# Moving the scalings of the Down weights inside a block, and re-ordering the first step with attention

## The chip, the cores and the metric

The kernel runs on one core of a Trainium2 chip. The core has five engines that follow their own queues of instructions: TensorE (PE in the profile; its weight loads are PEld), VectorE (DVE), ScalarE (ACT), GpSimd (POOL) and SyncE (SP), which here issues the transfers. The metric is the device time of one execution in microseconds, as the median of several runs.

## The reference

A layer mixes two branches by a gate. Tokens: 2048, width 576, 32 heads of 18, four segments of 512 tokens, hidden width 4608:

```python
g = sigmoid((x * gate_w).sum(-1, keepdims=True))
a = A(x, wq, wk, wv, wo, beta)                # causal softmax attention inside each segment, mixed per
                                              # head with a read of a memory summed over earlier segments
b = (gelu(x @ w_gate) * (x @ w_up)) @ w_down  # GEGLU feed-forward
return g * a + (1 - g) * b
```

Attention in a segment is `softmax(q k^T * scale + mask) @ v`; the memory adds `phi(k)^T v` of each segment for the later ones.

## The kernel before, in words

**Words and scales.** All large products are made of float16 words: each float32 operand is scaled by a power of two and split into a high word and the low word that is left, and a product is three matmuls (high by high, high by low, low by high). The scale comes from the sum of squares of the operand.

**Blocks and steps.** After a first part (projections, memory), the main loop runs over 72 steps v (`step`, L1455). The 4608 hidden columns are 36 slices of 128; two slices make a block fb (18 blocks of four steps, i4 = 0 to 3), and a step takes one slice f = v // 2 and one half of the tokens (two chunks of 512). "Third step" below means i4 = 2, the first step of a block's second slice. Each step forms gate and up values for two chunks by a scheme with seven block products instead of eight; its operands are sums of weight blocks and sums of token blocks, and its results are built up in three banks called V, X (bank G) and Y (bank U). Y starts as a copy of X (L1504 in the first two steps of a block, L1507 in the others), X and Y are then continued with different products (`product`, L533; `rest` and `half_rest` for the last 64 columns of the width). VectorE reads Y twice on the way (L1558 or L1560 for the first chunk, L1598 for the second) and V once (L1606); a product that goes on in a bank waits until VectorE has read it. ScalarE makes the GELU (L1323), VectorE the gated value (`hidden`, L1305), ScalarE its high word (L1312), GpSimd its low word (L1320).

**The nested product.** In the fourth step of a block and the first of the next, one of the seven products is itself made by such a scheme, with 256 columns a matmul (`nest`, L1408, four parts n = 0 to 3 in one bank V of two halves). VectorE copies and adds between the parts: L1421 after part 0, L1424 and L1425 after part 1 (part 2 goes on in both halves that L1425 reads and writes), L1429 after part 2, L1432 after part 3. In the first block this happens with `at = (1, 1)` in step v = 4.

**Down products.** The hidden values of block fb - 1 are multiplied with its Down weights during block fb: 32 chains of six matmuls with 288 columns (`down`, L1272, by `chains` / `some`), eight in a step, five of them "early", three "late". Each chain ends in one of two dn banks and VectorE adds it to the result (L1290; L1288 in block 1).

**Attention.** From v = 4 on, step v carries one head of one half sequence, k = v - 4, for 64 steps (`on(k)`): the scores of two segments (`scores`, L1170, matmuls L1190, in banks dn, st and pv), VectorE's masked maxima (L1196, started by `put`), the exponentials and words on ScalarE and GpSimd (`powers`, L1203: L1210, L1214, L1215, L1216), transposes by SyncE (L1219), the products with v (`values`, L1221, bank pv) and `normalize` (L1236, last instruction L1250). The scores of step k need bank pv after `normalize` of k - 2 has read it.

**Preparation of weights.** While a block runs, the weights of the next are scaled on VectorE (`scale_g`, L314), summed on GpSimd (`sums_g`, L337 to L342; `nest_odd`, `nest_pairs`, `nest_sums`, L375 to L397) and split (`high_g`, L348 on ScalarE; `low_g`, L352 on GpSimd). The Down weights of the block itself (`raw_d`, two slices) come in during its first step, ScalarE sums their squares in its second (L89), `scale_d` (L399, instruction L401) scales them in place on VectorE, `high_d` (L403, instruction L405) makes the upper half on ScalarE, `low_d` (L407, instruction L409) the lower half on GpSimd in the fourth step. They are used from the next block on.

**Order.** The order of the instructions on TensorE, ScalarE, VectorE and GpSimd is the order in which the code emits them (a manual schedule); semaphores are set from the data that they share. SyncE's transfers go in order too. So a line's place in `step` is its place in its engine's queue: `weights_nest(fb, i4, 2)` is the end of a step, and `end_pair` (L1443) the start of the next.

Of the kernel before, what the change touches and what calls it, by code (L numbers as in the profile page):

```python
# [27 lines left out]
NB = NF // 2  # L28
# [15 lines left out]
def kernel(ctx: ExitStack, tc: tile.TileContext, xs, wqk, wv, wo, wgu, wd, beta, out):  # L44
# [234 lines left out]
    def scales_rest(fb):  # L279
        z, pb = scl_a[fb]  # L280
        dve.tensor_scalar(pb[:, 0, 0:2].bitcast(I32), z[:, 4:6].bitcast(I32), 1, EXP, OP.logical_shift_right, OP.bitwise_and)
        dve.tensor_scalar(pb[:, 0, 2:6].bitcast(I32), z[:, 0:4].bitcast(I32), EXP, None, OP.bitwise_and)
        dve.tensor_scalar(pb[:, 1].bitcast(I32), pb[:, 0].bitcast(I32), EXP, None, OP.bitwise_xor)
# [24 lines left out]
    A11, A12, U4, A22, G4, S1, UG, S2, S4 = 0, 2, 4, 5, 7, 8, 10, 11, 13  # L308
    KW = KT * P

    def scale_g(f, cols=slice(0, KT * P)):
        if f < NF:
            r = raw_g[f].rearrange("p (a b) -> p a b", a=2)[:, :, cols]
            dve.tensor_scalar(r, r, scl[f // 2][0][:, 0:1], None, OP.mult)  # L314
# [16 lines left out]
    def sums_g(f):  # L331
        if f >= NF:
            return
        r = raw_g[f]
        g0, g2, u0, u2 = (r[:, o : o + 2 * P] for o in (0, 2 * P, KW, KW + 2 * P))
        g4, u4 = r[:, 4 * P : KW], r[:, KW + 4 * P :]
        pool.tensor_tensor(g2, g0, g2, OP.add)  # L337
        if f < 2 or f % 2 == 0:
            pool.tensor_tensor(g0, u0, g0, OP.subtract)
        pool.tensor_tensor(u0, g2, u0, OP.subtract)  # L340
        pool.tensor_tensor(u2, u2, u0, OP.subtract)
        pool.tensor_tensor(g4, u4, g4, OP.subtract)  # L342
# [23 lines left out]
    def nest_part(b):  # L366

        w = nest_w[b][:, 10 * P :].bitcast(F32)
        return raw_g[2 * b][:, : 2 * P], w

    def nest_odd(b):
        if b < NB:
            nest_w[b] = nest_tile()
            r = raw_g[2 * b + 1]
            pool.tensor_tensor(nest_part(b)[1], r[:, KW : KW + 2 * P], r[:, : 2 * P], OP.subtract)  # L375

    def nest_pairs(b, i, what):
        if b >= NB:
            return
        a, r = nest_part(b)  # L380
        src, o = ((a, W00), (r[:, P:], W11), (r, WS3), (a, WS2))[i]
        n = src.shape[1]
        hi, lo = (nest_w[b][:, (o + 7 * j) * P : (o + 7 * j) * P + n] for j in range(2))
        if "h" in what:
            act.activation(hi, src, AF.Copy)
        if "l" in what:
            pool.tensor_tensor(lo, src, hi, OP.subtract)
# [11 lines left out]
    def scale_d(f):  # L399
        r = raw_d[f]  # L400
        dve.tensor_scalar(r, r, scl[f // 2 + 1][0][:, 1:2], None, OP.mult)  # L401

    def high_d(f):  # L403
        t = pair_d[f] = home["d"].tile([P, 2, D], F16, name="paird", tag="paird", bufs=4)
        act.activation(t[:, 0], raw_d[f], AF.Copy)  # L405
# [127 lines left out]
    def product(o, f, a, x, h, l, start=False, ks=(0, 1)):  # L533

        w = pair_g[f]
        for k in ks:
            for i, b in ((0, h), (0, l), (1, h)):
                pe.matmul(o, w[:, i, (a + k) * P : (a + k + 1) * P], x[:, b + k],  # L538
                          start=start and k == 0 and i == 0 and b == h, stop=k == 1 and i == 1,
                          skip_group_check=True)  # L540
# [20 lines left out]
    with tc.tile_pool(name="prj", bufs=2, side="right", reuse_waits="tile") as pp:  # L561
# [262 lines left out]
        with tc.manual_schedule(engines=ORDERED):  # L824
# [43 lines left out]
            x1 = [pp.tile([P, L], F32, name="phi", bufs=9) for _ in range(2)]  # L868
# [253 lines left out]
    with tc.tile_pool(name="keep", bufs=2, side="right", reuse_waits="tile") as kp, ExitStack() as tail:  # L1122
# [222 lines left out]
                scale_g(n0 + 2)  # L1345

        def weights_nest(fb, i4, at):
            if i4 == 1 and at == 2 and 0 < fb < NB - 1:
                for f in (2 * fb, 2 * fb + 1):
                    scale_d(f)  # L1350
            if i4 == 2 and at == 1:
                if fb:
                    scale_g(2 * fb + 3, FRONT)
                    sums_g(2 * fb + 2)
                nest_odd(fb + 1)
            if i4 == 2 and at == "late":
                for i in range(2):
                    nest_pairs(fb + 1, i, "hl")
                nest_sums(fb + 1)
            if i4 == 2 and at == 2:  # L1360
                for i in (2,) if fb else (2, 3):
                    nest_pairs(fb + 1, i, "hl")
            if i4 == 3 and at == 0 and fb:
                nest_pairs(fb + 1, 3, "hl")

        def weights_high(fb, i4):
            n0 = 2 * fb
            high_g(n0 + 1 + i4 // 2, i4 % 2)
            if i4 >= 2:
                high_d(n0 + i4 - 2)  # L1370

        def weights_low(fb, i4):
# [35 lines left out]
        def nest(at, n):  # L1408

            if at is None:  # L1410
                return
            b, p = at
            if n == 0:
                nested[at] = bank("V")
                holds[p] = kp.tile([P, L], F32, name=f"hold{p}", bufs=1)
            B, A = (nested[at][:, i * HX : (i + 1) * HX] for i in range(2))
            h0, h1 = (holds[p][:, i * HX : (i + 1) * HX] for i in range(2))
            if n == 0:
                nest_product(b, B, W00, X00, p, True)
                nest_product(b, A, WS3, XT3, p)  # L1420
                dve.tensor_copy(h1, A)  # L1421
            if n == 1:
                nest_product(b, A, W11, XT4, p)
                dve.tensor_copy(h0, A)  # L1424
                dve.tensor_copy(A, B)  # L1425
            if n == 2:
                nest_product(b, B, W01, X10, p)
                nest_product(b, A, WS2, XT2, p)
                dve.tensor_tensor(h0, A, h0, OP.add)  # L1429
            if n == 3:  # L1430
                nest_product(b, A, WS1, XT1, p)
                dve.tensor_tensor(h1, A, h1, OP.add)  # L1432
# [22 lines left out]
        def step(v):  # L1455

            f, p = divmod(v, 2)
            fb, i4 = divmod(v, 4)
            c, e = 2 * p, 2 * p + 1
            k = v - LAG  # L1460
            on = lambda i: 0 <= i < 2 * H
            early = range(8 * i4, 8 * i4 + 5)
            late = range(8 * i4 + 5, 8 * i4 + 8)
            some = lambda b, js: chains(b, js) if b >= 0 else None
# [4 lines left out]
            x1, x2_, t = x16[c], x16[e], xt[p]  # L1469
# [8 lines left out]
            at = (fb + 1, 0) if i4 == 3 and fb + 1 < NB else (fb, 1) if i4 == 0 and fb else None  # L1478
# [7 lines left out]
            X, Y = bank("G"), bank("U")  # L1486
# [88 lines left out]
                scales_out(fb + 1)  # L1575
            if both and i4 != 1:
                normalize(k - 2)
            product(X, f, A12, x1, 2, 6, ks=(0,) if on(k) else (0, 1))
            if v != 3 and not on(k):
                rest(X, f, U4, x1, (0,) if fb else (0, 1))  # L1580
            if fb > 1 and i4 == 1:
# [7 lines left out]
                rest(X, f, U4, x1)  # L1589
            if on(k):  # L1590
                scores(k, (f, V, G4, x1, 0), (f, X, U4, x1, 0), (f, Y, G4, x2_, 64))
                product(X, f, A12, x1, 2, 6, ks=(1,))
                rest(X, f, U4, x1, (0,))
            elif fb:
                low_rests(f, (V, G4, x1), (Y, G4, x2_))
# [16 lines left out]
            if on(k) and i4 == 1:  # L1612
                scales_sum(fb + 1, pool)
                scales_rest(fb + 1)
            rear = list(early[3 + (v == 4) :])
            if not on(k):
                some(fb - 1, rear)
# [18 lines left out]
            if on(k):  # L1636
                some(fb - 1, rear[:-1])
                nest(at, 0)
                some(fb - 1, rear[-1:])
                nest(at, 1)  # L1640
                put(2 * k + 1, 1)
                puts.pop(2 * k)
                weights_nest(fb, i4, "late")
                powers(2 * k)
                some(fb - 1, late[:1])
                ends.append((f, c, X, g0))
                end_first()
                some(fb - 1, late[1:2])
                nest(at, 2)
                some(fb - 1, late[2:])  # L1650
                if on(k - 1):
                    values(2 * k - 2)
                nest(at, 3)
            else:
                if v != 3:
                    nest(at, 0)
                some(fb - 1, late[:1])
                if v != 3:
                    nest(at, 1)
                weights_nest(fb, i4, "late")  # L1660
                some(fb - 1, late[1:])
                if v != 3:
                    nest(at, 2)
                if fb:
                    low_rests(f, (X, U4, x1), (Y, UG, x2_))
                    ends.append((f, c, X, g0))
                    if at or i4 == 1:
                        end_first()
                if on(k - 1):
                    values(2 * k - 2)  # L1670
                if v != 3:
                    nest(at, 3)
# [160 lines left out]
        with tc.manual_schedule(engines=ORDERED):  # L1833
# [17 lines left out]
            fb = NB - 1  # L1851
            for t in range(turned_n, 9):
                turned(t)
            for t in range(16):
                for n in range(2):
                    down(fb, t, n)
                if t in (1, 4):
                    f, c, o, g = ends.pop(0)
# [82 lines left out]
```

## Time and profile before

| | |
|---|---|
| Runs before | 1564.15, 1564.54, 1564.54 us (median 1564.54) |
| Profiled execution | 1564.22 us, span 1562.1 us |
| TensorE (PE) busy | 1550.3 us, 99% of the span |
| VectorE (DVE) busy | 1257.6 us, 81% |
| ScalarE (ACT) busy | 1210.0 us, 77% |
| GpSimd (POOL) busy | 1123.9 us, 72% |
| Granted TensorE clock | 1.000 |

Rows of a timeline read: start in us from the span's start, duration in us, engine, line of the kernel, operation, output tile <- input tiles, partitions x elements and type, and x with the number of instructions that the row merges. In square brackets stands the time that the engine was idle before the row and what ended it. Rows of the waits read: engine, tile and line that waited <- what it waited for: total us, times, longest us. The row of one line's instructions gives the shortest, median and longest duration in ns, then the first and the last start. Since matmuls are pipelined, the duration of a matmul row includes time in which the next one already runs; the distance between two starts is the pace.

### The profile page before, as it was taken

Reading aid. Unit: us, or ns where it says so; the run is one execution under the profiler, and the core shown is the slowest. Engines: PE = TensorE matmul, PEld = TensorE weight load, DVE = VectorE, ACT = ScalarE, POOL = GpSimd, SP = SyncE. Lnnn points to the kernel's source line nnn. Section 1 sums busy time; section 2 is a strip of 40 time slices with the busy share of each in tenths; the row PEclk is TensorE's granted clock in tenths of the full one; section 3 lists DMA queues with packets and bytes.
Section 4 is the critical chain, followed back from the end, with each engine's and each line's share of the span. In section 5 each row is a group of like instructions: output and inputs, shape, how many; then the busy total and the mean of one; then the engine's idle time right before and its main releaser. Section 6 shows DMA issues by size and latency. Waiting matters only on the chain. (4 is left out here: it accounts for less than half of the span.)

```text
span 1562.1 us, 33442 instructions
## 1 busy us (share of the span) xinstructions
PE 1550.3 (99%) x12196; PEld 967.7 (62%) x12196; DVE 1257.6 (81%) x3222; ACT 1210.0 (77%) x2059; POOL 1123.9 (72%) x1233
## 2 busy tenths in 40 slices
PE   9999999999999999999999999999999999999999
PEld 5765655565656666666666565666666666656577
DVE  7878986888888888888788888888888878887675
ACT  7567545898989888888889888989888888877421
POOL 4355566777777778686877777777878686777597
PEclk9999999999999999999999999999999999999999
DMA  7644441465747576656656584757576666655646
GB/s 246 235 153 146 155 133 41 106 133 102 146 109 149 112 154 119 138 127 124 135 117 136 107 154 106 149 111 165 113 146 123 123 139 126 129 104 102 122 91 168
DMA packets 483477, 206.69 MB, mean 132 GB/s; under 512 B 427248, under 2 KB 462320, under 8 KB 482800
## 3 DMA queue, kind: packets, MB, share of 16 engines
q1 hardware_dynamic: 483312, 204.56, 58.6%
q8 instruction: 95, 1.56, 0.4%
q14 instruction: 70, 0.57, 0.1%
HBM read 83.91 MB, written 31.98 MB: 74 GB/s over the span
## 5 line engine op out<-in xcount | busy, mean ns | idle before, releaser
L538 PEld LDWEIGHTS <-pairg 128*128 128x128 f16 x2592 | 242.5, 97 | 266.0 <-issue 23.8
L1280 PE MATMUL dn<-paird,hhr 128*128 128x288 f16 x2115 | 329.9, 286 | 0.2
L1290 DVE SCALAR_TENSOR_TENSOR acc<-dn,ev,acc 128x288 f32<-128x288 f32 x533 | 267.6, 513 | 76.8 <-PE dn L1280 74.4
L1214 ACT ACTIVATE pb<-pb,mb,esc 128x512 f32<-128x512 f32 (+3 forms) x512 | 304.9, 642 | 5.3
L1216 POOL TENSOR_TENSOR pb<-pb,ph 128x896 f16<-128x896 f32 (+1 forms) x128 | 187.7, 1467 | 118.6 <-ACT ph L1215 94.7
L1216 POOL TENSOR_TENSOR pl<-pb,ph 128x896 f16<-128x896 f32 (+1 forms) x128 | 180.6, 1431 | 120.4 <-ACT ph L1215 120.4
L1280 PEld LDWEIGHTS <-hhr 128*128 128x128 f16 x2160 | 210.2, 98 | 74.5 <-issue 1.3
L538 PE MATMUL G<-x,pairg 128*128 128x512 f16 x864 | 221.0, 380 | 0.0
L538 PE MATMUL U<-xt,pairg 128*128 128x512 f16 x864 | 209.9, 379 | 4.5 <-DVE U L1507 4.3
L1280 PE MATMUL dn<-paird,hhd 128*128 128x288 f16 x1275 | 208.7, 286 | 0.0
L1215 ACT ACTIVATE ph<-pb 128x896 f16<-128x896 f32 (+1 forms) x256 | 188.6, 737 | 9.6
L352 POOL TENSOR_TENSOR pairg<-raw,pairg 128x384 f16<-128x384 f32 (+2 forms) x144 | 157.6, 1115 | 17.2 <-ACT pairg L348 17.2
L1280 PEld LDWEIGHTS <-hhd 128*128 128x128 f16 x1296 | 125.6, 98 | 47.4 <-issue 0.5
L1405 PE MATMUL V<-xt,nest 128*128 128x256 f16 x714 | 105.5, 272 | 0.6 <-DVE hold L1429 0.4
L538 PE MATMUL U<-x,pairg 128*128 128x512 f16 x432 | 105.0, 379 | 0.0
L538 PE MATMUL V<-x,pairg 128*128 128x512 f16 x426 | 103.3, 378 | 0.1
L1196 DVE CUSTOM_DVE_ANT_0 pb<-st,mask 128x128 f32<-128x128 f32 (+2 forms) x192 | 96.5, 503 | 0.0
L1323 ACT ACTIVATE gl<-gl,sc 128x512 f32<-128x512 f32 x110 | 75.2, 712 | 26.0 <-DVE gl L1598 13.7
L1196 DVE CUSTOM_DVE_ANT_0 pb<-dn,mask 128x512 f32<-128x512 f32 (+2 forms) x192 | 92.1, 505 | 0.0
L1233 PEld LDWEIGHTS <-pt 128*128 128x128 f16 x2560 | 83.3, 96 | 6.5 <-issue 0.2
L419 PEld LDWEIGHTS <-wp 128*128 128x128 f16 x504 | 48.8, 98 | 59.0 <-DVE wp L115 1.0
L348 ACT ACTIVATE pairg<-raw 128x384 f16<-128x384 f32 (+2 forms) x144 | 77.8, 587 | 8.9 <-DVE raw L314 6.5
(367 smaller groups left out, 3213.7 us busy)
## 6 DMA issues: line engine op xcount, KB each, us to landing
raw<-in_wgu_dram SPq DMA_DIRECT2D x36, 640.0 KB
qkt<-qk SPq DMA_DIRECT2D x192, 108.0 KB
rawd<-in_wd_dram SPq DMA_DIRECT2D x36, 288.0 KB
qk<-stage SPq DMA_DIRECT2D x32, 256.0 KB
qk<-stage SPq DMA_DIRECT2D x40, 128.0 KB
vp<-vstage SPq DMA_DIRECT2D x16, 296.0 KB
vt<-vp SPq DMA_DIRECT2D x16, 296.0 KB
orow<-oa SPq DMA_DIRECT2D x16, 288.0 KB
```

The costliest lines, as they stand in the source:

```text
L348: act.activation(spot(f, *p, 0), raw_g[f][:, p[0] : p[1]], AF.Copy)
L352: pool.tensor_tensor(spot(f, *p, 1), raw_g[f][:, p[0] : p[1]], spot(f, *p, 0), OP.subtract)
L538: pe.matmul(o, w[:, i, (a + k) * P : (a + k + 1) * P], x[:, b + k], start=start and k == 0 and i == 0 and b == h, stop=k == 1 and i == 1, ...
L1196: dve.tensor_tensor_reduce(scored(u, qi), out[u, qi], mask[:, L - (qi + 1) * P :], 1.0, -3e38, OP.add, OP.max, mx[u][:, qi : qi + 1])
L1214: act.activation(r, r, AF.Exp, bias=b[:, qi : qi + 1], scale=esc[:, 0, c : c + 1])
L1215: act.activation(h[:, cols], p, AF.Copy)
L1216: pool.tensor_tensor(low[:, cols], p, h[:, cols], OP.subtract)
L1233: pe.matmul(ov, pr[:, 10 * i + COL[qi] // P + kb], v[:, 4 * e + kb, c0 : c0 + VC], start=kb == 0 and i == 0, stop=kb == qi and i == 1)
L1280: pe.matmul(o[:, :NH], hh[:, a, q * P : (q + 1) * P], w[:, b, n * NH : (n + 1) * NH], start=i == 0, stop=i == 5)
L1290: dve.scalar_tensor_tensor(av, o[:, :NH], ev, av, OP.mult, OP.add)
L1323: act.activation(t, o, AF.Gelu_apprx_tanh, scale=scl[f // 2][0][:, 2 + c : 3 + c])
L1405: pe.matmul(o, w[:, (7 * c + i) * P : (7 * c + i + 1) * P], x[d], start=start and n == 0, stop=n == 2, skip_group_check=True)
```

## The change

Three things are moved; no computation is added or taken away.

- In blocks 1 to 16, the two scalings of the block's Down weights (`scale_d`) leave the end of the second step. The first of them stands in the third step behind the maxima of the scores, the second at the third step's end.
- In the same blocks, the upper half of the first Down slice (`high_d(2 * fb)`) moves from the middle of the third step to its end. The second slice's stays in the fourth step, as do both lower halves. The last block keeps its order.
- In the first step with attention (v = 4, k = 0), X's second group of three matmuls stands right behind the first, ahead of the scores, and the first "late" Down chain stands ahead of part 1 of the nested product instead of behind it.

```diff
         def weights_nest(fb, i4, at):
-            if i4 == 1 and at == 2 and 0 < fb < NB - 1:
-                for f in (2 * fb, 2 * fb + 1):
-                    scale_d(f)
             if i4 == 2 and at == 1:
...
             if i4 == 2 and at == 2:
                 for i in (2,) if fb else (2, 3):
                     nest_pairs(fb + 1, i, "hl")
+                if 0 < fb < NB - 1:
+                    high_d(2 * fb)
+                    scale_d(2 * fb + 1)
             if i4 == 3 and at == 0 and fb:
                 nest_pairs(fb + 1, 3, "hl")
 
         def weights_high(fb, i4):
             n0 = 2 * fb
             high_g(n0 + 1 + i4 // 2, i4 % 2)
-            if i4 >= 2:
+            if i4 == 3 or (i4 == 2 and fb == NB - 1):
                 high_d(n0 + i4 - 2)
...
-            product(X, f, A12, x1, 2, 6, ks=(0,) if on(k) else (0, 1))
+            product(X, f, A12, x1, 2, 6, ks=(0,) if k > 0 and on(k) else (0, 1))
...
             if on(k):
                 scores(k, (f, V, G4, x1, 0), (f, X, U4, x1, 0), (f, Y, G4, x2_, 64))
-                product(X, f, A12, x1, 2, 6, ks=(1,))
+                if k:
+                    product(X, f, A12, x1, 2, 6, ks=(1,))
                 rest(X, f, U4, x1, (0,))
...
             if on(k) and i4 == 1:
                 scales_sum(fb + 1, pool)
                 scales_rest(fb + 1)
+            if on(k) and i4 == 2:
+                scale_d(2 * fb)
...
                 some(fb - 1, rear[:-1])
                 nest(at, 0)
                 some(fb - 1, rear[-1:])
+                if k == 0:
+                    some(fb - 1, late[:1])
                 nest(at, 1)
                 put(2 * k + 1, 1)
                 puts.pop(2 * k)
                 weights_nest(fb, i4, "late")
                 powers(2 * k)
-                some(fb - 1, late[:1])
+                if k:
+                    some(fb - 1, late[:1])
```

## The prediction

> **What bounds the kernel now.** I read the page's head first, then the waits of TensorE, then the timeline of one block of the steady part (block 12, whose third step begins near 1092 us) engine by engine.
>
> ```profile
> span 1562.1 us, 33442 instructions
> ```
>
> The profiled execution took 1564.22 us, so 2.1 us lie around the span; the three runs have 1564.15, 1564.54 and 1564.54, so my sum, made against 1564.22, may read 0.3 us low against the median. TensorE is busy 99% of the span. What a re-ordering can win is therefore only what TensorE still waits for.
>
> ```profile
> PE U L538 <- DVE U L1507: 4.3, 16, 0.8
> ...
> PE V L1405 <- DVE hold L1429: 0.4, 1, 0.4
> ```
>
> One wait comes back 16 times, once in each block from 1 to 16: product Y of the third step waits for the copy of X into Y's bank. Idle time understates it, because a matmul's modelled end overlaps the next start. I therefore measure from start to start:
>
> ```profile
> 1093.75 1.46 PE L538 MATMUL G<-x,pairg 128*128 128x512 f16 x6
> ...
> 1096.28 0.38 PE L1328 MATMUL V<-x,pairg 128*128 128x512 f16 x1
> 1096.89 1.46 PE L538 MATMUL U<-xt,pairg 128*128 128x512 f16 x6 [0.23 <-DVE U L1507]
> ...
> 1101.91 0.39 PE L1332 MATMUL V<-x,pairg 64*128 64x512 f16 x1
> 1102.33 0.27 PE L1190 MATMUL pv<-qkt 54*128 54x256 f16 x1
> ...
> 1105.69 3.91 PE L1280 MATMUL dn<-paird,hhd 128*128 128x288 f16 x30
> ...
> 1113.77 0.38 PE L1328 MATMUL V<-x,pairg 128*128 128x512 f16 x1
> 1113.98 1.46 PE L538 MATMUL U<-xt,pairg 128*128 128x512 f16 x6
> ...
> 1119.01 0.39 PE L1332 MATMUL V<-x,pairg 64*128 64x512 f16 x1
> 1119.23 0.27 PE L1190 MATMUL pv<-qkt 54*128 54x256 f16 x1
> ```
>
> The fourth step (last four rows) shows the undisturbed pace: 0.21 us from V's rest to Y, 0.22 us from the half rest to the first score. The third step needs 0.61 and 0.42 us. So two stalls stand in each third step: 0.40 us at the copy, and 0.20 us at the scores, which no wait of the table names. VectorE is behind both:
>
> ```profile
> 1092.59 0.51 DVE L401 TENSOR_SCALAR rawd<-rawd,sc 128x576 f32<-128x576 f32 x1
> 1093.02 2.15 DVE L401 TENSOR_SCALAR rawd<-rawd,sc 128x576 f32<-128x576 f32 x1
> ...
> 1096.14 0.70 DVE L1507 COPY U<-G 128x512 f32<-128x512 f32 x1
> ...
> 1098.25 0.88 DVE L314 TENSOR_SCALAR raw<-raw,sc 128x1280 f32<-128x1280 f32 x1
> 1099.05 0.68 DVE L1558 TENSOR_TENSOR gl<-U,hold 128x512 f32<-128x512 f32 x1
> ...
> 1101.88 0.30 DVE L1250 TENSOR_TENSOR ob<-ob,pv 128x144 f32<-128x144 f32 x1
> ...
> 1105.01 0.42 DVE L1196 CUSTOM_DVE_ANT_0 pb<-pv,mask 128x256 f32<-128x256 f32 x1
> ...
> 1106.63 0.52 DVE L1290 SCALAR_TENSOR_TENSOR acc<-dn,ev,acc 128x288 f32<-128x288 f32 x1 [1.18 <-PE dn L1280]
> ...
> 1112.73 0.70 DVE L1507 COPY U<-G 128x512 f32<-128x512 f32 x1 [1.70 <-PE G L538]
> ```
>
> The two scalings of the Down weights hold VectorE for 2.5 us ahead of the third step; it then shows no idle time until 1106, so the copy is late, and so is the last normalizing instruction (L1250, which reads the bank that the first score overwrites: it ends at 1102.18, the score begins 0.15 us later). Where the two scalings go, VectorE has idle time: 1.18 us behind the scores' maxima and 1.70 us before the fourth step's copy.
>
> **The scalings leave the second step's end.** The copy then waits for X alone. X's six matmuls begin at 1093.75 and end near 1095.2, the copy (0.70 us) near 1095.95; Y's natural start is 1096.28 + 0.21 = 1096.49, so 0.5 us are to spare and the stall goes whole: 15 blocks by 0.40 us is 6.0 us. The first block's is larger:
>
> ```profile
> 262.89 0.81 PE L538 MATMUL G<-x,pairg 128*128 128x512 f16 x3
> 263.91 1.46 PE L538 MATMUL U<-xt,pairg 128*128 128x512 f16 x6 [0.21 <-DVE gl L1560]
> ...
> 272.93 0.53 PE L1280 MATMUL dn<-paird,hhr 128*128 128x288 f16 x3
> 273.30 0.53 PE L1280 MATMUL dn<-paird,hhd 128*128 128x288 f16 x3
> 274.22 0.49 PE L1405 MATMUL V<-xt,nest 128*128 128x256 f16 x3 [0.39 <-DVE hold L1429]
> ...
> 295.38 0.38 PE L1328 MATMUL V<-x,pairg 128*128 128x512 f16 x1
> 296.58 1.46 PE L538 MATMUL U<-xt,pairg 128*128 128x512 f16 x6 [0.82 <-DVE U L1507]
> ```
>
> In block 1 (last two rows) 1.20 - 0.21 = 0.99 us; together 7.0 us. Bounds: none of it (if VectorE is still held) and all 7.0; I take all, since the cover is 0.5 us.
>
> **What of the scores' stall goes with it.** With the copy at 1095.25 instead of 1096.14, VectorE is 0.89 us ahead when it comes to the scaling of L314 (1097.36). That one may meet GpSimd:
>
> ```profile
> 1095.90 2.27 POOL L1320 TENSOR_TENSOR hhr<-gl,hhr 128x512 f16<-128x512 f32 x2
> 1101.22 2.88 POOL L1216 TENSOR_TENSOR pb<-pb,ph 128x896 f16<-128x896 f32 x2 [3.06 <-ACT ph L1215]
> 1104.07 2.27 POOL L352 TENSOR_TENSOR pairg<-raw,pairg 128x640 f16<-128x640 f32 x2
> 1106.42 0.73 POOL L337 TENSOR_TENSOR raw<-raw 128x256 f32<-128x256 f32 x1
> ```
>
> GpSimd's two low halves run until 1098.17, or about 0.25 us less where no scaling comes between. What such a meeting costs is in the pair of scalings itself:
>
> ```profile
> 1092.93 1.91 POOL L1216 TENSOR_TENSOR pl<-pb,ph 128x896 f16<-128x896 f32 x1 [1.99 <-ACT ph L1215]
> ```
>
> The same scaling takes 0.51 us or 2.15 us. The long one starts at 1093.02, while GpSimd is in its 896-column subtraction, and ends at 1095.17, 0.33 us behind it. GpSimd's next subtraction stood ready in the same queue, so a scaling waits out the GpSimd instruction it meets, and only that one. L314 then ends near 1098.55 (alone, near 1098.2): VectorE is 0.5 us ahead of before (0.9 at best), and L1250 ends near 1101.68. TensorE, 0.40 us ahead, would have its score at 1101.91 - 0.40 + 0.22 = 1101.73 and gets it at 1101.68 + 0.15 = 1101.83. Of 0.20 us, 0.10 is left: gain 0.10 by 16 blocks, 1.6 us. Bounds 0 (VectorE gains no more than TensorE) and 3.2; I take 1.6, as the GpSimd row stands where L314 arrives.
>
> The Trainium skill (SBUF — State Buffer, section "Who interferes with whom") states this as a rule: VectorE in a two-port mode and GpSimd share one pair of SBUF ports, whoever issues first has it for the whole instruction, and the other fully blocks. The two durations, 0.51 and 2.15 us, agree. The rule speaks against the change in so far as it makes the price of a moved scaling a matter of what GpSimd is doing there; by the rule, with a subtraction issued first behind the scores, the sum would be that of the slower rival below, and with VectorE first the forecast's.
>
> **The first scaling, behind the scores.** VectorE comes to it when the last maximum ends, at 1105.43 by before, some 0.5 us earlier now, at 1104.93. Queued behind it is the eviction of the first Down chain (1106.63 of before). That eviction has no slack to give: with two dn banks the third chain starts 1.47 us behind 1105.69, at 1107.16, and 1106.63 + 0.52 is 1107.15. So what the scaling holds beyond 1106.63 - 0.50 = 1106.13 is paid by TensorE one to one. GpSimd sets it. Its L352 pair follows ScalarE's exponentials, which begin as soon as the maxima are there:
>
> ```profile
> 1098.37 0.30 ACT L1210 ACTIVATE mb<-mx,esc 128x4 f32<-128x4 f32 x1
> ...
> 1103.52 0.67 ACT L405 ACTIVATE paird<-rawd 128x576 f16<-128x576 f32 x1
> ...
> 1133.85 0.30 ACT L1210 ACTIVATE mb<-mx,esc 128x4 f32<-128x4 f32 x1 [1.19 <-DVE mx L1196]
> ```
>
> With VectorE 0.89 us ahead there, the L352 pair ends near 1105.45 instead of 1106.34, and the scaling is through 0.3 us later, at 1105.75: 0.4 us before it matters. I take 0. Bounds: 0, and a scaling of 2.15 us that has just missed a long subtraction, 1104.93 + 2.15 - 1106.13 = 0.95 us a block.
>
> **The second scaling, at the third step's end.** Before it VectorE stood idle for 1.70 us; 2.15 us at worst makes the copy 0.45 us late, to 1113.18, done at 1113.88, before Y at 1113.98. Cost 0 at either bound; without the idle time it would be the old stall again.
>
> **The upper half.** 0.67 us of ScalarE moves from before the GELU (1103.52) to behind the third step's sums. ScalarE then runs without idle time into the next block, where it waits 1.19 us for VectorE at 1133.85: that hides 0.67. The lower half that needs it, and frees the raw buffer for the next load, stays in the fourth step; no moved instruction issues a transfer, and SyncE's queue keeps its order. Cost 0; uncovered, it would delay a GELU by 0.67 us.
>
> **The first step with attention.** Moving X's last three matmuls (0.65 us) ahead of Y's next product removes the wait at 263.91: 262.89 and three paces of 0.21 make 263.53, so 0.38 us. The moved Down chain leaves only one chain (0.74 us, twice 272.93 to 273.30) between parts 1 and 2 of the nested product where two stood. Part 2 waits for both copies behind part 1:
>
> ```profile
> 271.11 0.41 DVE L1424 COPY hold<-V 128x256 f32<-128x256 f32 x1
> 271.56 0.43 DVE L1425 COPY V<-V 128x256 f32<-128x256 f32 x1
> ```
>
> From part 1's end they need 0.2 us until the result is readable (as an eviction behind its chain), 0.1 us behind the moved chain's eviction, and 0.45 + 0.48: 1.23 us, of which 0.74 are covered; 0.50 us are new. Part 3 then waits some 0.35 us where it waited 0.55 (274.22 against 273.30 + 0.37). Sum: -0.38 + 0.50 - 0.20 = -0.1 us. Bounds -0.9 (both waits of before gone) and +0.5.
>
> **Sum.** 7.0 + 1.6 + 0.1 = 8.7 us: 1564.22 - 8.7 = 1555.5 us.
>
> **The rivals.** *GpSimd does not move ahead with VectorE* (its chain is fed by ScalarE, which also squares the next weights there). Then the scaling behind the scores is through at 1106.34 + 0.3 = 1106.6 and the eviction is 0.47 us late, 16 times: 7.5 us back of 8.7, so 1563.0; where GpSimd comes half-way, 1559.3. For it: ScalarE's queue is dense. Against it: the 3.06 us for which GpSimd waited before 1101.22.
>
> *The change does not free the copy.* VectorE would have to be held at 1094 by something else, L1305 waiting for a late GELU, say. Then 0 to 1 us: 1564. Against it: VectorE's 2.57 us are gone and its other work there is evictions of finished banks.
>
> *Slower: the scaling behind the scores meets the 896-column subtraction.* If GpSimd's L1216 pair (2.88 us from 1101.22) starts some 2 us later in the new order, the scaling waits it out: 0.95 us a block at worst, 15.2 us, and the gain of 8.7 stays: 1564.22 + 6.5 = 1570.7. It decides from 0.55 us a block on, that is, from a scaling through after 1106.7. For it: the second scaling of each old pair paid exactly this. Against it: L1216 would have to slip past L352's old place, while all that feeds it comes earlier.
>
> **How the numbers follow.** Chances: forecast 0.66 (1553.7 with all of the scores' stall, to 1557.6 with none of it and 0.5 us lost in the first step); GpSimd late 0.16, half of it still under 1561; copy not freed 0.08; slower 0.07; rest 0.03. From no change I tell 0.2%, 3.1 us. Faster: 0.66 + 0.08 + part of the rest and of the half-way cases, 0.79; same 0.14; slower 0.07. The range goes from 1553.7 to 1561: the forecast and the half-way cases of the first rival.
>
> **What would show it.** Right: no wait of Y on L1507 in the third steps; V's rest to Y 0.21 us; half rest to score under 0.35 us; the scaling behind the scores through before its eviction's chain has ended, L401 under 1.2 us; the fourth step's copy still waiting for X. Wrong: an idle TensorE between the second and third Down chain behind the scores, L401 at 2 us there, or a new wait on L1425 in the first step over 0.6 us.

## The result, and the profile after

The changed kernel takes 1554.61 us (1554.51 to 1555.19, four runs) where the kernel before took 1564.35 us on the same chip (1563.44 to 1564.54, four runs): 9.7 us less, a ratio of 0.9940 with a 95% interval of 0.9922 to 0.9957. The profiled execution took 1554.51 us against 1564.22 us: 9.7 us less, 9.3 of them inside the span and 0.4 around it. The forecast was 1555.5 us.

The page's head and TensorE's waits of the changed kernel:

```profile
span 1552.8 us, 33427 instructions
```

```profile
PE G L829 <- POOL onesb L825: 1.0, 1, 1.0
...
PE V L1405 <- DVE V L1425: 0.3, 1, 0.3
...
PE V L1405 <- DVE hold L1429: 0.2, 1, 0.2
```

The row of Y's wait for the copy (L1507, 16 times) is gone from the table. In the first step, the row on L1425 is new and the one on L1429 has gone from 0.4 to 0.2 us. The only other row that the table before lacks is one of 0.2 us at an eviction in block 1 (L1288), a wait that is about the same in both from start to start (0.31 and 0.32 us). TensorE's timeline from the same block as before (its third step begins near 1085 us now; the last two rows are the fourth step):

```profile
1089.36 0.38 PE L1328 MATMUL V<-x,pairg 128*128 128x512 f16 x1
1089.57 1.46 PE L538 MATMUL U<-xt,pairg 128*128 128x512 f16 x6
...
1094.59 0.39 PE L1332 MATMUL V<-x,pairg 64*128 64x512 f16 x1
1094.88 0.27 PE L1190 MATMUL pv<-qkt 54*128 54x256 f16 x1
...
1098.24 3.91 PE L1280 MATMUL dn<-paird,hhd 128*128 128x288 f16 x30
...
1106.31 0.38 PE L1328 MATMUL V<-x,pairg 128*128 128x512 f16 x1
1106.53 1.46 PE L538 MATMUL U<-xt,pairg 128*128 128x512 f16 x6
```

V's rest to Y is 0.21 us in the third step now, as in the fourth: the copy's stall is gone whole. Half rest to first score is 0.29 us, where 0.42 stood and 0.22 is free of any wait. The Down chains behind the scores run through as one row of 30 matmuls, so the scaling that now stands there makes no matmul wait. VectorE and GpSimd in the same stretch:

```profile
1088.32 0.70 DVE L1507 COPY U<-G 128x512 f32<-128x512 f32 x1 [1.70 <-PE G L538]
...
1090.44 1.25 DVE L314 TENSOR_SCALAR raw<-raw,sc 128x1280 f32<-128x1280 f32 x1
...
1094.43 0.30 DVE L1250 TENSOR_TENSOR ob<-ob,pv 128x144 f32<-128x144 f32 x1
...
1097.91 0.93 DVE L401 TENSOR_SCALAR rawd<-rawd,sc 128x576 f32<-128x576 f32 x1
1099.17 0.52 DVE L1290 SCALAR_TENSOR_TENSOR acc<-dn,ev,acc 128x288 f32<-128x288 f32 x1 [0.33 <-PE dn L1280]
...
1102.62 0.66 DVE L401 TENSOR_SCALAR rawd<-rawd,sc 128x576 f32<-128x576 f32 x1
...
1105.28 0.70 DVE L1507 COPY U<-G 128x512 f32<-128x512 f32 x1 [1.12 <-PE G L538]
```

```profile
1088.73 2.27 POOL L1320 TENSOR_TENSOR hhr<-gl,hhr 128x512 f16<-128x512 f32 x2
1093.41 2.88 POOL L1216 TENSOR_TENSOR pb<-pb,ph 128x896 f16<-128x896 f32 x2 [2.41 <-ACT ph L1215]
1096.25 2.28 POOL L352 TENSOR_TENSOR pairg<-raw,pairg 128x640 f16<-128x640 f32 x2
1098.61 0.82 POOL L337 TENSOR_TENSOR raw<-raw 128x256 f32<-128x256 f32 x1
```

The copy has 1.70 us of idle VectorE ahead of it and waits for X alone. L314 takes 1.25 us instead of 0.88, because GpSimd's two L1320 run until 1091.00 there: this is what is left of the scores' stall, since L1250 ends at 1094.73 and the score begins 0.15 us behind it, as before. Behind the scores, GpSimd's L352 pair ends at 1098.53, the scaling is through at 1098.84, and VectorE is idle for another 0.33 us until the first Down chain has ended. The fourth step's copy still waits for X, 1.12 us.

### The profile page after: what moved, and what is told of

The parts are those of the page before. It is cut to its first block, busy times and chain, and to the rows that moved or that the text cites. A ratio compares the mean times of both kernels' runs of the same rounds, so it can differ in the third digit from the quotient of the medians.

```text
span 1552.8 us, 33427 instructions
## 1 busy us (share of the span) xinstructions
PE 1545.9 (100%) x12196; PEld 967.2 (62%) x12196; DVE 1251.1 (81%) x3222; ACT 1208.7 (78%) x2059; POOL 1123.1 (72%) x1233
## 3 DMA queue, kind: packets, MB, share of 16 engines
q8 instruction: 95, 1.56, 0.4%
## 4 chain that ended last, share of the span: by engine, by line
PE 94%; DVE 2%; ACT 1%; POOL 1%; DMA 1%; issue 0%; SPq 0%; POOLq 0%; ACTq 0%; DVEq 0%
PE dn L1280 26%; PE U L538 17%; PE G L538 12%; PE V L538 6%; PE V L1405 5%; PE pv L1233 4%; PE U L1328 3%; PE st L419 3%; PE dn L426 2%; PE U L419 1%; PE G L419 1%; PE U L1332 1%; PE st L1786 1%; PE st L1190 1%; PE V L1328 1%; PE G L1328 1%
## 5 line engine op out<-in xcount | busy, mean ns | idle before, releaser
L1216 POOL TENSOR_TENSOR pb<-pb,ph 128x896 f16<-128x896 f32 (+1 forms) x128 | 185.5, 1450 | 112.4 <-ACT ph L1215 93.2
L1216 POOL TENSOR_TENSOR pl<-pb,ph 128x896 f16<-128x896 f32 (+1 forms) x128 | 177.0, 1404 | 119.4 <-ACT ph L1215 119.4
L352 POOL TENSOR_TENSOR pairg<-raw,pairg 128x384 f16<-128x384 f32 (+2 forms) x144 | 157.8, 1117 | 17.2 <-ACT pairg L348 17.2
```

What stands on the lines that cost most here:

```text
L352: pool.tensor_tensor(spot(f, *p, 1), raw_g[f][:, p[0] : p[1]], spot(f, *p, 0), OP.subtract)
L1216: pool.tensor_tensor(low[:, cols], p, h[:, cols], OP.subtract)
```

## The experiments

The theory at the start: all of the gain is VectorE being free earlier in the third step; the price of the old place was the meeting with GpSimd's 896-column subtraction, not the scalings' own work; the first step's re-ordering is worth nothing. The rivals: the two scalings' own time, or the new places as such, or the first step, carry a part of it. "The kernel before" was measured again beside each group of runs and took 1564.13 to 1564.20 us there.

**The weights alone.** The first step's edits are undone.

```diff
-            product(X, f, A12, x1, 2, 6, ks=(0,) if k > 0 and on(k) else (0, 1))
+            product(X, f, A12, x1, 2, 6, ks=(0,) if on(k) else (0, 1))
...
-                if k == 0:
-                    some(fb - 1, late[:1])
                 nest(at, 1)
...
-                if k:
-                    some(fb - 1, late[:1])
+                some(fb - 1, late[:1])
```

> The changed kernel without its two edits in the first step with attention; only the scalings and the upper half are moved. Theory (all of the gain is the two stalls of the third steps): 9.2 to 9.8 us faster than before, within 0.3 us of the changed kernel; in the first step the waits of before, 0.38 and 0.56 us from start to start. Rival (the first step carries a part): 0.5 us or more of the gain is missing.

Measured: 1554.91 us (1554.77 to 1555.12), ratio 0.9941 (0.9926 to 0.9956). The first step's waits of before are back in its table:

```profile
PE V L1405 <- DVE hold L1429: 0.4, 1, 0.4
...
PE U L538 <- DVE gl L1560: 0.2, 1, 0.2
```

That is 9.2 us under the kernel before beside it, of the 9.7 us of the whole change. From the first Down chain to its last matmul's end TensorE takes 1293.4 us here and 1293.5 in the changed kernel, where it took 1302.7 before. So the weights' part carries the gain.

**The first step alone.** The same edits, made to the kernel before.

> The kernel before with only the two edits of the first step. Theory: 0 to 0.2 us faster; the wait of 0.38 us on L1560 is gone, 0.5 us are new ahead of part 2 of the nested product (on L1425), 0.35 us are left ahead of part 3 (on L1429) where 0.56 stood; the 16 waits of the third steps stay, 0.40 us each and 0.99 in block 1. Rival: the reordering frees more than it costs, 0.9 us faster.

Measured, in a single run: 1563.7 us, span 1561.6 us against 1562.1. The copy's wait stays, and the new short row of the first step appears:

```profile
PE U L538 <- DVE U L1507: 4.2, 16, 0.8
...
PE V L1405 <- DVE V L1425: 0.3, 1, 0.3
```

Half a microsecond in a single run is no effect that can be told from none, as expected. Start to start, the step loses its 0.37 us at Y and gets 0.51 us ahead of part 2, while part 3's wait goes from 0.56 to 0.36 us.

**One scaling stays.** From the changed kernel: the first scaling goes back to the second step's end and the upper half to its old place; only the second scaling has moved.

```diff
         def weights_nest(fb, i4, at):
+            if i4 == 1 and at == 2 and 0 < fb < NB - 1:
+                scale_d(2 * fb)
...
                 if 0 < fb < NB - 1:
-                    high_d(2 * fb)
                     scale_d(2 * fb + 1)
...
             high_g(n0 + 1 + i4 // 2, i4 % 2)
-            if i4 == 3 or (i4 == 2 and fb == NB - 1):
+            if i4 >= 2:
                 high_d(n0 + i4 - 2)
...
-            if on(k) and i4 == 2:
-                scale_d(2 * fb)
```

> The first scaling stays at the second step's end and the upper half in the middle of the third step; only the second scaling moves, to the third step's end; nothing stands behind the scores. Theory (the meeting with GpSimd's long subtraction is the price, not the scaling's own work): the scaling that stays takes 0.51 us, is through before the subtraction starts, both stalls of the third step go as in the changed kernel (copy 0, scores under 0.1 us), time within 0.5 us of the changed kernel, 1554 to 1555.2. Rival (the place behind the scores is what brings it, since every scaling costs about 1.25 us wherever it stands): the scores' stall stays at 0.15 to 0.2 us, time 1556.5 to 1558.

Measured: 1555.48 us (1555.32 to 1555.94), ratio 0.9945 (0.9929 to 0.9962). VectorE and GpSimd around it:

```profile
1086.44 0.51 DVE L401 TENSOR_SCALAR rawd<-rawd,sc 128x576 f32<-128x576 f32 x1
...
1089.09 0.70 DVE L1508 COPY U<-G 128x512 f32<-128x512 f32 x1 [1.27 <-PE G L538]
```

```profile
1086.77 2.79 POOL L1216 TENSOR_TENSOR pl<-pb,ph 128x896 f16<-128x896 f32 x2 [1.99 <-ACT ph L1215]
```

The scaling that stays begins 0.33 us before GpSimd's subtraction, takes 0.51 us, and VectorE is idle for 1.27 us ahead of the copy: no stall is left there. With the 0.89 us by which the copy had been late (1096.14 against 1095.25 in the prediction), 2.16 us of VectorE came free by moving one scaling that takes 0.51 us by itself. So neither the place nor the first scaling was the price, but the second one, which came behind the start of the subtraction. The time is 0.3 us above the expected upper end; of the 0.9 us between the two profiled executions, 0.4 are in the scores' gaps (0.31 to 0.32 us instead of 0.28 to 0.31 in 15 blocks, and 0.31 instead of 0.22 in block 1). Another 0.2 us lie ahead of the first Down chain and 0.4 around the span, where the two kernels are the same.

**Half of the second scaling.** In the kernel before, the second scaling covers 288 of the 576 columns; the other 288 are left unscaled.

```diff
-    def scale_d(f):
-        r = raw_d[f]
+    def scale_d(f, n=D):
+        r = raw_d[f][:, :n]
...
-                for f in (2 * fb, 2 * fb + 1):
-                    scale_d(f)
+                scale_d(2 * fb)
+                scale_d(2 * fb + 1, NH)
```

> The kernel before, the second scaling of a block on 288 of its 576 columns (the others stay unscaled, so a part of the computation is left out). Theory (it waits for GpSimd): its duration falls by no more than its own work, 2.15 to about 2.0 us; the copy's stall falls from 0.40 to about 0.25 us; 2 to 3 us faster. Rival (the time is the scaling's own work): half of 2.15, about 1.1 us; the copy's stall is gone; 7 to 9 us faster.

Measured, in a single run: 1561.96 us, 2.2 us under the kernel before. The row of L401 (shortest, median and longest in ns), and the halved scaling of block 12:

```profile
L401 DVE TENSOR_SCALAR rawd<-rawd,sc x36: 507/998/2066, 225.4 to 1457.3; 128x576 f32<-128x576 f32 x20, 128x288 f32<-128x288 f32 x16
```

```profile
1091.50 2.00 DVE L401 TENSOR_SCALAR rawd<-rawd,sc 128x288 f32<-128x288 f32 x1
```

Half the columns still cost 2.00 us instead of 2.15, in 15 of the 16 blocks: nearly all of that duration is waiting. (The longest of the row, 2.07 us, covers all 576 columns. In block 1 both scalings come behind the start of the subtraction, here and in the kernel before, and the first one has the long duration there.) The copy's stalls, summed start to start, fall by 2.4 us, from 6.9 to 4.5 us; the time of the single run shows 2.2. Had the work been the price, its half would have taken most of the stall away. The Trainium skill's rule (SBUF — State Buffer, section "Who interferes with whom"), that the one that issues second is blocked fully, agrees with both this pair of durations and the 0.51 us above.

**Both scalings behind the scores.**

```diff
                 if 0 < fb < NB - 1:
                     high_d(2 * fb)
-                    scale_d(2 * fb + 1)
...
             if on(k) and i4 == 2:
                 scale_d(2 * fb)
+                scale_d(2 * fb + 1)
```

> Both scalings behind the maxima of the scores. Theory (what stands there beyond 0.33 us of idle time is paid one to one, since the eviction of the first Down chain has no slack): the first scaling takes 0.93 us, the second meets GpSimd's next sum (L337, 0.82 us) and holds VectorE until about 0.5 us behind the time at which the eviction could start (0.4 to 0.75); TensorE waits that long between the second and the third Down chain of each third step, 16 times, 6.5 to 12 us: 1561 to 1566.6. Rival (the eviction has slack, or the second scaling does not meet GpSimd): within 1 us of the changed kernel.

Measured: 1562.11 us (1561.77 to 1562.62), ratio 0.9987 (0.9978 to 0.9997): 7.5 us of the gain are given back. TensorE, VectorE and the wait that makes it:

```profile
1104.07 1.63 PE L1280 MATMUL dn<-paird,hhd 128*128 128x288 f16 x12
1106.05 2.40 PE L1280 MATMUL dn<-paird,hhd 128*128 128x288 f16 x18 [0.35 <-DVE acc L1290]
```

```profile
1103.74 1.83 DVE L401 TENSOR_SCALAR rawd<-rawd,sc 128x576 f32<-128x576 f32 x2
1105.49 0.93 DVE L1290 SCALAR_TENSOR_TENSOR acc<-dn,ev,acc 128x288 f32<-128x288 f32 x2
```

```profile
PE dn L1280 <- DVE acc L1290: 5.2, 15, 0.4
```

The two scalings are through at 1105.57; the third chain needs the eviction that starts then, and begins at 1106.05, 1.98 us behind the first. In the changed kernel it begins 1.51 us behind the first. That is 0.47 us a block and 7.5 us over 16 blocks: the eviction behind the scores has no slack beyond what one scaling uses. The place takes one scaling free of charge and not two.

**Both at the third step's end.** `scale_d(2 * fb)` ahead of the upper half there, nothing behind the scores.

> Both scalings at the third step's end, none behind the scores. Theory: the first takes about 0.66 us, the second waits out one of GpSimd's short instructions there (0.7 us) and ends 0.2 to 0.4 us before the fourth step's copy could start; no new wait, time within 0.5 us of the changed kernel. Rival (the stall moves into the fourth step's copy): 0.1 us or more from V's rest to Y beyond 0.21 us in each fourth step, 2 us or more.

Measured, in a single run: 1554.66 us, span 1552.9 us. The only row in the waits that the changed kernel hasn't is one of 0.4 us on a transfer (L721), ahead of the main loop. The two scalings take 1.35 us together, and VectorE is still idle ahead of the fourth step's copy:

```profile
1105.44 0.70 DVE L1508 COPY U<-G 128x512 f32<-128x512 f32 x1 [0.42 <-PE G L538]
```

So this run shows no difference between the two free places.

**The first step in another order.** The late chain stands behind part 1 again, and one maximum moves behind part 2, so that VectorE's two copies behind part 1 come sooner.

```diff
-                if k == 0:
-                    some(fb - 1, late[:1])
                 nest(at, 1)
-                put(2 * k + 1, 1)
+                if k:
+                    put(2 * k + 1, 1)
...
-                if k:
-                    some(fb - 1, late[:1])
+                some(fb - 1, late[:1])
...
                 some(fb - 1, late[1:2])
                 nest(at, 2)
+                if not k:
+                    put(2 * k + 1, 1)
```

> The changed kernel with the late Down chain of the first step back behind part 1 of the nested product, and one maximum of the scores (the second unit's second) moved behind part 2. Theory (two Down chains between parts 1 and 2 cover the copies, and VectorE's queue between them is what part 3 waits for): no wait ahead of part 2, about 0.2 us ahead of part 3 instead of 0.50 and 0.36: 0.65 us less in the first step, 0.4 to 0.8 us off the span. Rival: part 3 waits 0.5 us as before the change, since its wait is not VectorE's order.

Measured, in a single run: 1553.46 us, span 1551.8 us; the rows of L1425 and L1429 are gone. Then in four runs, beside the changed kernel once more:

> The other order of the first step, timed: 0.6 to 1.2 us under the changed kernel, as its waits before parts 2 and 3 of the nested product, 0.50 and 0.36 us, are gone.

> The changed kernel once more, beside the next two on one chip: 1554.5 to 1555.2 us.

Measured: 1554.32 us (1553.93 to 1554.52) against 1554.55 us (1554.25 to 1555.05) for the changed kernel. Part 2 waits no more and part 3 0.21 us instead of 0.36, which makes 0.65 us. From the first Down chain to TensorE's end it is 1292.9 us in both profiles of this order, and 1293.4 and 1293.5 in the two of the changed kernel: the 0.5 to 0.6 us are there. The medians differ by 0.2 only, not by the 0.6 to 1.2 us expected, and don't resolve it, because the part ahead of that chain differs by up to 1.1 us between the four profiles (255.5 to 256.6 us), where these kernels are the same.

**The low half later.** From the changed kernel: the low half of the third step's first hidden value (one of the two L1320 that L314 meets) is put off, to free L314 and the scores.

```diff
-                end_pair(i4 == 3 and fb > 0)
+                end_pair(i4 >= 2 and fb > 0)
```

> The changed kernel with the low half of the third step's first hidden value made later on GpSimd, behind the lower halves of the weights, as the fourth step does. Theory (what is left of the scores' stall, 0.07 us, comes from L314 meeting L1320): L314 on 1280 columns takes 0.88 us instead of 1.25, the scores' stall is gone, 1 us faster than the changed kernel, if GpSimd's later work in the step, 1.1 us later, still hides. Rival: that shift reaches TensorE in the fourth step, 1 us or more slower than the changed kernel.

Measured: 1569.97 us (1569.55 to 1570.31), ratio 1.0038 (1.0024 to 1.0052), 15.4 us slower than the changed kernel. The stall aimed at is gone: L314 takes 0.89 us and the scores' gap is 0.22 us everywhere. The price stands in the fourth step, in VectorE, GpSimd and the waits:

```profile
1125.62 2.32 DVE L1263 SCALAR_TENSOR_TENSOR ob<-ob,wsc,oh 128x576 f16<-128x576 f32 x1
...
1131.30 0.75 DVE L1305 SCALAR_TENSOR_TENSOR gl<-G,sc,gl 128x512 f32<-128x512 f32 x1 [0.36 <-ACT gl L1323]
```

```profile
1125.44 3.28 POOL L1216 TENSOR_TENSOR pb<-pb,ph 128x896 f16<-128x896 f32 x2 [1.46 <-ACT ph L1215]
```

```profile
PE V L1405 <- DVE hold L1421: 8.0, 15, 0.5
PE V L1405 <- DVE hold L1429: 4.9, 17, 0.9
```

L1263, which has both inputs in SBUF, comes 0.18 us behind the start of GpSimd's first subtraction and takes 2.32 us. In the changed kernel it comes 1.56 us behind it, near its end, and takes 0.94 us; the two engines' rows there:

```profile
1114.81 0.94 DVE L1263 SCALAR_TENSOR_TENSOR ob<-ob,wsc,oh 128x576 f16<-128x576 f32 x1
```

```profile
1113.25 3.28 POOL L1216 TENSOR_TENSOR pb<-pb,ph 128x896 f16<-128x896 f32 x2 [1.46 <-ACT ph L1215]
```

With the low half later, the copies behind the nested product's part 0 (L1421) are late by that, and a later gated value waits for its GELU. Start to start, over all blocks, TensorE loses 10.0 us ahead of part 1 and 6.5 us ahead of part 3, and wins 1.1 us at the scores: 15.4 us, which is the whole difference. The mechanism is that of the prediction's slower rival, at another instruction and another place. That GpSimd's later sums and ScalarE's later chain bring the meeting about is read from the order of the rows (L1320 alone at 1109.36, ahead of L337 at 1110.70) and was not tried by itself.

**Both further.** The first step's other order, and the scaling of L314 moved ahead of the third step's copy, into the idle time that the change opened there.

```diff
             else:
+                if fb and i4 == 2:
+                    scale_g(2 * fb + 2)
                 dve.tensor_copy(Y, X)
...
-            if i4 == 2:
-                scale_g(n0 + 2)
```

> The other order of the first step, and the scaling of the next block's weights (L314 on 1280 columns) moved ahead of the third step's copy, where VectorE has 1.70 us of idle time. Theory: it waits out GpSimd's 896-column subtraction there, to about 0.2 us behind the copy's time in the changed kernel, which the 0.5 us of cover take; L1250 comes 0.5 us earlier, the rest of the scores' stall (0.07 us, 15 times) is gone, 1 us under the other order alone. Rival: the copy becomes late again, or the maxima, and with them ScalarE's exponentials, 0.2 us later, push the two-input instruction L1263 of each fourth step into GpSimd's long subtraction: L1263 over 1.3 us, new waits on L1421, 1 to 17 us slower.

Measured: 1552.67 us (1552.49 to 1553.41), ratio 0.9928 (0.9914 to 0.9941): 1.9 us under the changed kernel beside it, the shortest of all these kernels.

```profile
1084.93 2.04 DVE L314 TENSOR_SCALAR raw<-raw,sc 128x1280 f32<-128x1280 f32 x1
1086.90 0.68 DVE L1507 COPY U<-G 128x512 f32<-128x512 f32 x1
```

```profile
1087.76 0.38 PE L1328 MATMUL V<-x,pairg 128*128 128x512 f16 x1
1087.97 1.46 PE L538 MATMUL U<-xt,pairg 128*128 128x512 f16 x6
...
1092.99 0.39 PE L1332 MATMUL V<-x,pairg 64*128 64x512 f16 x1
1093.21 0.27 PE L1190 MATMUL pv<-qkt 54*128 54x256 f16 x1
```

L314 meets GpSimd there too, takes 2.04 us, and costs nothing: the copy ends at 1087.58, 0.39 us before Y's natural start. The scores' gap is 0.22 us in all blocks. The two parts add up: 15 times 0.07 us of the scores' stall and 0.65 us of the first step make 1.7 us, of 1.9 measured.

## Why the prediction was right, point by point

**The bound, and the measure.** Reading from start to start was right, and needed: the table's 4.3 us at L1507 stood for 6.9 us of stall. TensorE's last matmul ends at 1549.47 instead of 1558.83 us, 9.4 us earlier. Of these, 9.2 us lie behind the start of the first Down chain, and the stalls named below add up to 9.2 us.

**The copy.** "The stall goes whole", 7.0 us: measured 6.9 (15 blocks by 0.39 us and 0.98 in block 1). The rival "the change does not free the copy" is out: 1.70 us of idle VectorE stand ahead of it.

**The scores' stall.** That no wait of the table names it was not quite right: the table before has one row for it, which is block 14's alone.

```profile
PE pv L1190 <- DVE ob L1250: 0.2, 1, 0.2
```

The mechanism was right: L314 now meets GpSimd's L1320, waits them out and ends behind them. The term was mis-sized: 1.6 us predicted, 2.2 measured. Of 0.20 us a block, 0.07 is left and not 0.10, since L1250 ends 0.14 us behind the half rest's start where I had 0.17; over 15 blocks that is some 0.4 us. Two blocks were not as the others: block 1 lost all of its 0.20 us, and block 14, counted as 0.20 us, had 0.33 us and lost 0.25 of it. The bounds, 0 to 3.2, held it.

**The first scaling behind the scores**, at 0: right, and by its own steps. Counted from the start of the Down chains, the L352 pair was to end 0.26 us behind it and does so at 0.29; the scaling was to be through at 0.56 and is at 0.60; it would begin to cost at 0.94. So the first rival, that GpSimd doesn't move ahead with VectorE, is out: GpSimd waited for ScalarE's words (2.41 us ahead of the L1216 pair), ScalarE for VectorE's maxima (0.57 us), and the whole chain moved:

```profile
1090.56 0.30 ACT L1210 ACTIVATE mb<-mx,esc 128x4 f32<-128x4 f32 x1 [0.57 <-DVE mx L1196]
```

The price that the rival had put on a late eviction is right, though: both scalings there made it 0.5 us late and cost 7.5 us.

**The second scaling and the upper half**, at 0: right. The copy behind them still waits 1.12 us for X, and with both scalings in that place the time is the same.

**The first step**, at -0.1 us: the new wait ahead of part 2 is 0.51 us where 0.50 was worked out, part 3's is 0.36 where 0.35 was; with 0.37 gone at Y it nets to -0.06 us. The runs without it and with it alone show no difference that can be told from none.

**The slower rival** did not come here, because GpSimd's L1216 pair ended before the scaling started. It was a fair rival: one deferred instruction on GpSimd brought the same meeting about at L1263, and with it 15.4 us.

**The sum.** 6.9 + 2.2 + 0.1 is 9.2 of the 9.3 us in the span. The remaining 0.4 us between the profiled executions lies around the span and was in no term. So the forecast was 0.9 us too high, by 0.6 us of the scores' term and by what lies around the span.

## What to carry to other kernels

When an instruction of one engine has two durations far apart, look at what the other engine runs when the long one starts: here a scaling of 0.51 us became 2.15 us, and the cure was to have it start before, or well after, that instruction, not to make it shorter. Price a moved instruction at its new place by the time it is *through* there, counted against the latest time its follower can stand, and look for the follower with no slack (the eviction between two banks) as well as for the idle time. Whatever makes an engine earlier or later also moves the meetings further down its queue, so look through the whole period of the loop for pairs that are now close.

## What the runs showed that was not expected

- An instruction with two inputs in SBUF waits for GpSimd as the scaling does: L1263 takes 0.81 us alone (0.82 in the median before), and 2.32 us behind a 896-column subtraction. The row in the run with the low half later, shortest, median and longest in ns:

```profile
L1263 DVE SCALAR_TENSOR_TENSOR ob<-ob,wsc,oh x16: 809/2317/2329, 394.0 to 1462.4; 128x576 f16<-128x576 f32 x16
```

  The Trainium skill has this in the section named above (SBUF — State Buffer, "Who interferes with whom"), for two SBUF inputs against a GpSimd instruction that reads SBUF; this row agrees. I had looked for meetings among the scalings only.
- GpSimd pays as well, though less: its L337 takes 0.82 us behind the scaling where it took 0.73, and its pair of subtractions 3.28 us instead of 2.88 where L1263 stands in between. In the changed kernel no wait of TensorE's table comes of it.
- A stall can be named by no wait: of the scores' stalls before, 0.20 us in 15 blocks and 0.33 us in one, the table had the one of 0.33 us alone, and the rest of 0.07 us stands in no row after. Only the distance between two starts, compared with the same pair in an undisturbed step, shows it.
